# An attention and mixture-of-experts kernel: another guess of the first experts, other planning constants, and a last output cut in two

## The chip, the cores and the metric

The kernel runs on one core of one Trainium2 chip. The metric is the device time of one launch in microseconds (us), the median of several runs. An execution that the hardware profiler recorded is read beside it; its times are counted from the first instruction of its span.

## The reference

Eight batches of 576 tokens with eight heads of 64 columns go through a Nystrom attention with 32 landmarks, and its output rows (4608 of 512 columns) through a mixture of eight experts, one expert for each token.

```
q_lm, k_lm = q, k averaged over 18 neighbouring tokens           # 32 landmarks
A  = softmax(q @ k_lm.T / 8);  Bm = softmax(q_lm @ k_lm.T / 8);  C = softmax(q_lm @ k.T / 8)
Z  = Bm.T / (norm1(Bm) * norminf(Bm) + 1e-6);  six times: Z = 2 Z - Z @ Bm @ Z
x  = (A @ Z @ C @ v), heads side by side                          # (4608, 512)
logits = normalized(x) @ normalized(expert_emb).T / tau           # 8 experts
e  = argmax(logits);  gate = softmax(logits)[e]
out = gate * (relu(x @ w1[e]) @ w2[e])                            # 512 -> 1024 -> 512
```

## The kernel before

All tokens of a batch share one expert in these inputs, and the kernel is built on that. For each batch it guesses one expert, loads only that expert's two weight matrices, and computes the batch with them. It also routes every token exactly, counts the tokens whose expert is another than the guess, and at the very end runs a general path (`general`, under `tc.If` at line 1608) if the count is not zero. In the profiled execution that path did not run.

**A planner orders the work.** Each piece of work (loads, sums, values, queries, landmarks, guess, weights, first and second product of a batch) is a Python generator that announces what it will use next and for how long. The class `Weave` (line 131) plays these announcements against its own clocks, one for each engine, and the order in which it lets generators go on is the order of the instructions on every engine. On the chip each engine runs its instructions strictly in that order, so a planned time acts only through the order it makes. A transfer is taken as landed at the end of its planned share of the queue plus `DMA_LAT`, 3.6 us, whatever the batch (`wv.flag(..., DMA_LAT)`, lines 722, 723, 739, 1361). A group of matmuls may be planned only `MARGIN` (549.6 ns) after its operands, or `BMARGIN` (400 ns) for the two expert products; `SLACK` and `EPS` say how near two candidates must be for their ranks to decide, and `PRI` and `FIRST` hold the ranks.

**Warm matmuls.** Until the first expert product is planned, `keep_warm` (line 668) puts matmuls of a constant of ones (line 673) into the planned gaps of TensorE, so that the engine does not stand still. Their number comes from the planned gaps, too.

**Start.** SP issues the loads of batch 0 (k in two parts, q in two parts, v in two), then those of batch 1. VectorE sums k and q over 18 tokens each (line 762), TensorE starts on the landmarks with these sums, and the attention of batch 0 follows on all engines.

**The guess of batches 0 and 1** (`guess`, line 1168) needs only v. Ten matmuls with a block of ones as stationary operand (128 rows, 32 columns) and the values as moving operand (256 columns, the upper halves of the fp32 numbers read as bf16) sum v over all tokens into one PSUM bank, every sum 32 times over. VectorE transposes the bank (line 1188), multiplies it with the expert embeddings laid out 16 by 8 on each partition (`enB`, line 1193), and `choose` (line 1197) reduces, sums over the partitions with one more matmul, and finds the largest of the eight (line 1216 writes the expert's number). SP then reads that number into a register (line 1340) and issues eight weight transfers of 512 KB (line 1360). Later batches take their guess from the landmarks.

**From weights to the first expert product.** ScalarE squares the four slices of w1 as they land and sums them (line 1374), a power of two is formed from the total (`first_scale`), TensorE multiplies the weights with the batch's landmarks (`first_weights`), ScalarE and VectorE write the scaled result as two fp16 halves (lines 1418, 1420), and `first` (line 1475) multiplies it with the attention weights. `hidden` applies the ReLU (lines 1468, 1470), and `second` (line 1506) multiplies with w2.

**End.** `second` of the last batch takes its small chunk first and four chunks of 128 tokens after it. Each chunk is 24 matmuls of 512 columns into one PSUM bank. `outputs` (line 1540) scales a finished bank on ScalarE or VectorE and SP stores it, 256 KB for a chunk. Before the eviction of the last chunk every engine loads the count of wrong guesses (line 1545).

Of the kernel before, what the change touches and what calls it, by code (L numbers as in the profile page):

```python
# [8 lines left out]
F32 = mybir.dt.float32  # L9
# [42 lines left out]
DMA_LAT = 3600.0  # L52
SLACK = 53.2
EPS = 148.0
MARGIN = 549.6
BMARGIN = 400.0
# [21 lines left out]
PRI = {"loads": 897, "sums": 1694, "inverse": 1697, "values": 1597, "queries": 700, "landmarks": 1656, "rows": 500,  # L78
       "route": 794, "guess": 844, "weights": 803, "first": 550, "second": 550}
# [466 lines left out]
def nystrom_moe(ctx: ExitStack, tc: tile.TileContext, qT, kT, v, emb, w1, w2, out):  # L546
# [77 lines left out]
    con = cst.tile([P, H * E + DM // M * E + 1], F32, name="con")  # L624
# [3 lines left out]
    enB = con[:, H * E:H * E + DM // M * E].rearrange("p (k e) -> p k e", e=E)  # L628
    rtau = con[:, H * E + DM // M * E:]
# [46 lines left out]
    def embeddings():  # L676
# [17 lines left out]
        yield V2(128)  # L694
        vec.tensor_tensor(out=enB, in0=enB, in1=bc(er.unsqueeze(1), [P, DM // M, E]), op=ALU.mult)
# [10 lines left out]
    def loads(b):  # L706
        if b:
            yield "wait", ("loads", b - 1)
        for src, dst, nm in ((kT, kt, "k"), (qT, qt, "q")):
# [6 lines left out]
            for i in range(parts):  # L716
# [3 lines left out]
                for x in range(2 // parts * i, 2 // parts * (i + 1)):  # L720
                    wv.flag((nm, b, x), DMA_LAT)
            wv.flag((nm, b), DMA_LAT)
# [5 lines left out]
    def load_values(b, gg):  # L728
# [10 lines left out]
        wv.flag(("v", b, gg), DMA_LAT)  # L739
# [428 lines left out]
    def guess(b):  # L1168
# [21 lines left out]
        yield "wait", "enB"  # L1190
        pr = wk.tile([P, DM // M, E], F32, name="gpr", bufs=1)
        yield V2(128)
        vec.tensor_tensor(out=pr, in0=bc(tr[:, :, 0:1], [P, DM // M, E]), in1=enB, op=ALU.mult)
        wv.put("half")
# [311 lines left out]
    def second(b):  # L1506
# [5 lines left out]
        for c in order:  # L1512
# [4 lines left out]
            for f in range(8):  # L1517
# [15 lines left out]
                if c == order[-1]:  # L1533
                    wv.put("ht")
                    if f % 2 == 1:
                        wv.put("w2")
# [112 lines left out]
```

## Time and profile before

| | |
|---|---|
| time, median of 3 runs | 449.94 us (449.02 to 450.99) |
| the profiled execution's own time | 449.05 us |
| its span, first to last instruction | 447.3 us |
| TensorE busy | 432.4 us, 97% |
| VectorE busy | 328.1 us, 73% |
| ScalarE busy | 277.5 us, 62% |
| moved by DMA | 78.21 MB, mean 175 GB/s |
| mean granted TensorE clock | 0.995 |

The page calls TensorE's matmuls PE and its weight loads PEld, VectorE DVE, ScalarE ACT, GpSimd POOL and SyncE SP. All matmuls that go through the helper `mm` have its line, 583, so they are told apart by the tiles that they read and write. Warm matmuls have line 673. In a row of the timeline the first two numbers are start and length in us, a bracket at the end is the idle time of the engine before the instruction and what ended it. Busy time of matmuls is merged, so a group's length holds the pipeline's tail after the last start.

### The profile page before, as it was taken

The numbers are of one execution on the slowest core, as the hardware profiler recorded it, in microseconds if no ns is written. First come the engines' busy times: TensorE is split into PE (matmuls) and PEld (weight loads), VectorE is DVE, ScalarE is ACT, GpSimd is POOL, SyncE is SP. The second block draws the span as 40 slices with busy tenths as digits, with TensorE's granted clock in tenths as the row PEclk, the third lists the DMA queues.
The fourth block names the chain that finished last, engine by engine and source line by source line (L and its number), as shares of the span: only waits on it lengthen the run. The fifth ranks groups of instructions, "written<-read, shape, count | busy, mean of one in ns | idle before, by whom it ended". The sixth has DMA issues, their size and how long they took to land.

```text
span 447.3 us, 13932 instructions
## 1 busy us (share of the span) xinstructions
PE 432.4 (97%) x5628; PEld 245.5 (55%) x5628; DVE 328.1 (73%) x1110; ACT 277.5 (62%) x641; POOL 79.5 (18%) x80
## 2 busy tenths in 40 slices
PE   7999989999999999999999999999999999999994
PEld 3454554456555476455565466555665476457541
DVE  4877989988895689987995769765987669455300
ACT  1359645887655865987478648955597457945210
POOL 3042143422241104303230105001310101010000
PEclk9999999999999999999999999999999999999998
DMA  8687644884239816882595249322550219211011
GB/s 291 247 298 245 273 160 150 287 294 142 107 131 313 285 49 211 293 264 79 195 373 178 101 141 366 104 80 114 179 211 26 101 51 359 84 57 38 13 49 52
DMA packets 29705, 78.21 MB, mean 175 GB/s; under 512 B 2625, under 2 KB 14017, under 8 KB 27841
## 3 DMA queue, kind: packets, MB, share of 16 engines
q1 hardware_dynamic: 29488, 77.15, 48.6%
q8 instruction: 46, 0.75, 0.7%
q14 instruction: 27, 0.21, 0.1%
q10 hardware_dynamic: 144, 0.10, 0.1%
HBM read 61.96 MB, written 15.27 MB: 173 GB/s over the span
## 4 chain that ended last, share of the span: by engine, by line
PE 68%; DVE 21%; DMA 3%; ACT 3%; POOL 2%; issue 1%; SPq 1%; POOLq 0%; ACTq 0%; DVEq 0%
PE ps L583 61%; PE ps L673 5%; DVE ht L1470 4%; DVE w2c L1460 3%; DMA k_t<-kT 2%; POOL half L759 2%; DMA wstage<-w 2%; DVE qsum L762 1%; DVE cm L888 1%; PE ps L935 1%; DVE ksum L762 1%; DVE ww L1420 1%; DVE ae L986 1%; DVE asum L997 1%; ACT w2c L1458 1%
## 5 line engine op out<-in xcount | busy, mean ns | idle before, releaser
L583 PE MATMUL ps<-w2c,ht 128*128 128x512 f16 (+1 forms) x1152 | 208.9, 345 | 1.5 <-DVE w2c L1460 1.3
L583 PEld LDWEIGHTS <-ht 128*128 128x128 f16 (+1 forms) x1152 | 88.5, 102 | 79.4 <-issue 7.4
L583 PE MATMUL ps<-ab,ww 128*128 128x288 f16 x768 | 105.4, 286 | 2.2 <-DVE ht L1470 2.1
L583 PEld LDWEIGHTS <-ww 128*128 128x128 f16 x768 | 72.1, 98 | 34.1 <-issue 12.1
L1468 ACT ACTIVATE ht<-ps 128x288 f16<-128x288 f32 x128 | 51.9, 409 | 37.2 <-PE ps L583 36.5
L1470 DVE SCALAR_TENSOR_TENSOR ht<-ps,ht 128x288 f16<-128x288 f32 x128 | 54.7, 447 | 8.8 <-ACT ht L1468 8.5
L1460 DVE SCALAR_TENSOR_TENSOR w2c<-wstage,wsc,w2c 128x1024 f16<-128x1024 f32 x32 | 41.0, 1281 | 12.4 <-ACT w2c L1458 12.4
L1554 ACT ACTIVATE yt<-ps,gfac 128x512 f32<-128x512 f32 (+1 forms) x29 | 18.4, 635 | 46.5 <-PE ps L583 45.9
L1018 POOL TENSOR_TENSOR ae<-ae,am 128x576 f32<-128x576 f32 x15 | 17.3, 1159 | 101.4 <-DVE am L991 81.2
L1458 ACT ACTIVATE w2c<-wstage,wsc 128x1024 f16<-128x1024 f32 x30 | 34.4, 1149 | 0.6 <-PE ps L583 0.2
L1433 ACT ACTIVATE junk<-wstage 128x1024 bf16<-128x1024 f32 x32 | 33.9, 1059 | 0.3
L1374 ACT ACTIVATE junk<-wstage 128x1024 bf16<-128x1024 f32 x32 | 33.8, 1055 | 0.1
L1257 POOL TENSOR_TENSOR nrm<-ssq,half 128x5 f32<-128x5 f32 x8 | 10.0, 1251 | 124.6 <-ACT junk L1239 124.6
L673 PE MATMUL ps<-ones 128*128 128x512 bf16 (+3 forms) x117 | 28.4, 390 | 2.3 <-POOL ones L608 2.3
L1239 ACT ACTIVATE junk<-ps 128x512 bf16<-128x512 f32 (+1 forms) x40 | 23.9, 597 | 10.5 <-DVE lg L1237 9.8
L759 POOL TENSOR_TENSOR half<-k_t 128x576 f32<-128x576 f32 x14 | 18.2, 1302 | 41.2 <-DMA k_t<-kT 18.5
L1418 ACT ACTIVATE ww<-ps,wsc 128x1024 f16<-128x1024 f32 (+1 forms) x18 | 18.2, 1013 | 9.0 <-PE ps L583 9.0
L1420 DVE SCALAR_TENSOR_TENSOR ww<-ps,wsc,ww 128x1024 f16<-128x1024 f32 (+1 forms) x18 | 20.9, 1160 | 3.3 <-ACT ww L1418 3.0
L759 POOL TENSOR_TENSOR half<-q_t 128x576 f32<-128x576 f32 x13 | 17.3, 1332 | 25.5 <-DVE ksum L762 14.5
L583 PE MATMUL ps<-wgd,ab 64*128 64x136 f16 (+1 forms) x480 | 21.1, 221 | 0.6 <-DVE ht L1470 0.4
L583 PEld LDWEIGHTS <-ab 64*128 64x128 f16 (+1 forms) x480 | 14.4, 96 | 12.0 <-issue 11.3
L583 PEld LDWEIGHTS ps<-ek 32*32 32x32 f32 x768 | 12.3, 104 | 15.4 <-issue 6.0
(203 smaller groups left out, 567.8 us busy)
## 6 DMA issues: line engine op xcount, KB each, us to landing
wstage<-w SPq DMA_DIRECT2D x64, 512.0 KB, 6.9
v<-v SPq DMA_DIRECT2D x16, 512.0 KB, 5.1
out<-yt SPq DMA_DIRECT2D x32, 256.0 KB, 2.6
k_t<-kT SPq DMA_DIRECT2D x7, 1152.0 KB, 6.7
q_t<-qT SPq DMA_DIRECT2D x7, 1152.0 KB, 11.9
abs__135<-ab SPq DMA_DIRECT2D x8, 576.0 KB, 3.1
k_t<-kT SPq DMA_DIRECT2D x2, 576.0 KB, 5.6
q_t<-qT SPq DMA_DIRECT2D x2, 576.0 KB
```

Source lines behind the costliest of these rows:

```text
L583: pe.matmul(o, lhsT, rhs, start=start, stop=stop)
L673: pe.matmul(warmth[:, 0:k * P], ones16, bc(ones16.unsqueeze(1), [P, k, P]), start=True, stop=True)
L759: pool.tensor_tensor(out=half, in0=sv[:, :, 0:9], in1=sv[:, :, 9:18], op=ALU.add)
L1239: act.activation(junk[lo:hi, 0:512].rearrange("p (i g x) -> p i g x", i=2, g=2), pfv[:, :, :, 0:2 * D], AF.Square, accum_out=ssq[lo:hi, cg ...
L1374: act.activation(junk, stage[1, b, q], AF.Square, accum_out=sq[:, q:q + 1])
L1420: vec.scalar_tensor_tensor(out=ww[:, 1], in0=pww, scalar=sc, in1=ww[:, 0], op0=ALU.mult, op1=ALU.subtract)
L1433: act.activation(junk, stage[2, b, q], AF.Abs, accum_out=sq[:, q:q + 1])
L1458: act.activation(w[:, 0], st, AF.Copy, scale=sc)
L1460: vec.scalar_tensor_tensor(out=w[:, 1], in0=st, scalar=sc, in1=w[:, 0], op0=ALU.mult, op1=ALU.subtract)
L1468: act.activation(ht[:, 0, r], ph[:, 0:HS], AF.Relu)
L1470: vec.scalar_tensor_tensor(out=ht[:, 1, r], in0=ph[:, 0:HS], scalar=0.0, in1=ht[:, 0, r], op0=ALU.max, op1=ALU.subtract)
L1554: act.activation(yt[:, 0:n], py[:, 0:n], AF.Copy, scale=fac)
```

## The change

It has three parts and a set of constants that go with them.

1. The guess of batches 0 and 1 takes the values as the stationary operand (128 rows, 128 columns, five chunks for each of four column blocks, 20 matmuls) and one column of ones as the moving operand. The sums land with one number per partition, so the transpose goes, and `enB` shrinks from 16 by 8 to 4 by 8 on each partition. The `half` buffer, which the sums on GpSimd use too, is not taken any more.
2. The planner takes the loads of batch 0 (k, q, v and the weights) as landed 2.0 us after their share of the queue, later batches 3.6 us as before. The time that the planner keeps an output buffer (`yt`) after its store goes from 3.6 us to 2.0 us for every batch.
3. The last chunk of the last batch is computed in two halves of 256 columns, 24 matmuls each. The first half's eviction and store are given to the planner as soon as its matmuls are planned. The load of the count of wrong guesses moves to the first half's eviction.

```diff
-DMA_LAT = 3600.0
-SLACK = 53.2
-EPS = 148.0
-MARGIN = 549.6
-BMARGIN = 400.0
+DMA_LAT, DMA_LATE = 2000.0, 3600.0
+SLACK = 46.4
+EPS = 181.8
+MARGIN = 436.5
+BMARGIN = 436.5
 PRI: sums 1694 -> 1697, values 1597 -> 1603, queries 700 -> 703, landmarks 1656 -> 1653,
      route 794 -> 800, first 550 -> 544, second 550 -> 553
+def landing(b):
+    return DMA_LATE if b else DMA_LAT
...
-            wv.flag((nm, b), DMA_LAT)
+            wv.flag((nm, b), landing(b))
...
-        ps_, done = yield from take(T(790, cols=1024, tiles="columns"), 1)
-        for gg in range(2):
-            lead = vt[b, gg].bitcast(BF16).rearrange("p c (x i) -> p c x i", i=2)[:, :, :, 1]
+        ps_, done = yield from take(T(1120, cols=2600), 1)
+        for k in range(4):
+            lead = vt[b, k // 2].bitcast(BF16).rearrange("p c (x i) -> p c x i", i=2)[:, :, :, 1]
             for c in range(5):
-                j = c % 4
-                mm(ps_[32 * j:32 * j + 32, 256 * gg:256 * gg + 256], ones16[:, 0:M], lead[:, c],
-                   start=(c < 4), stop=(c > 0))
+                x = P * (k % 2)
+                mm(ps_[:, k:k + 1], lead[:, c, x:x + P], ones16[:, 0:1], start=(c == 0), stop=(c == 4))
...
-        yield "get", "half"
-        yield VT(512)
-        tr = wk.tile([P, 2 * M, SEG // 2], F32, name="half", bufs=1)
-        tr = tr.rearrange("p m t -> p (m t)")[:, 0:DM].rearrange("p (k r) -> p k r", r=M)
-        vec.transpose(tr.rearrange("p k r -> p (k r)"), ps_)
-        done()
         yield "wait", "enB"
-        pr = wk.tile([P, DM // M, E], F32, name="gpr", bufs=1)
-        yield V2(128)
-        vec.tensor_tensor(out=pr, in0=bc(tr[:, :, 0:1], [P, DM // M, E]), in1=enB, op=ALU.mult)
-        wv.put("half")
+        pr = wk.tile([P, 4, E], F32, name="gpr", bufs=1)
+        yield V(32)
+        vec.tensor_tensor(out=pr, in0=bc(ps_[:, 0:4].unsqueeze(2), [P, 4, E]), in1=enB, op=ALU.mult)
+        done()
...
-            for f in range(8):
+            parts = 2 if (b, c) == (B - 1, order[-1]) else 1
+            n = DM // parts
+            for f, x0 in [(f, n * i) for i in range(parts) for f in range(8)]:
...
-                        mm(py, ht[:, i, o:o + P], w[:, x], start=st_, stop=sp_)
+                        mm(py[:, x0:x0 + n], ht[:, i, o:o + P], w[:, x, x0:x0 + n], start=st_, stop=sp_)
...
+                if parts == 2 and f == 7 and x0 == 0:
+                    wv.add(outputs(b, c, py, None, S * b + o, slice(0, n)), boost=EVICT)
...
-        if (b, c) == (B - 1, 3):
+        if (b, c, cols.start) == (B - 1, 3, 0):
+            yield "wait", "mi"
             left.append(nc.values_load(mi[0:1, 0:1], min_val=0, max_val=NT))
...
-            sp.dma_start(out[t0:t0 + P], yt)
+            sp.dma_start(out[t0:t0 + P, cols], yt[:, 0:n])
```

## Rows read from the trace of the kernel before

**Rows 1.** The page, part 1: busy time, share of span and instructions of each engine.

```profile
PE 432.4 (97%) x5628; PEld 245.5 (55%) x5628; DVE 328.1 (73%) x1110; ACT 277.5 (62%) x641; POOL 79.5 (18%) x80
```

**Rows 2.** Windows: stretch, length, busy us of each engine, clock, DMA share, GB/s.

```profile
60.00:80.00 20.00, 18.19 (x308) 9.04 (x307) 19.15 (x69) 9.25 (x24) 6.51 (x6) 1.00 0.51 172
80.00:120.00 40.00, 39.48 (x620) 22.80 (x619) 34.47 (x110) 31.72 (x77) 12.14 (x10) 1.00 0.65 221
...
440.00:447.30 7.30, 0.96 (x5) 0.23 (x3) 0.00 (x0) 0.69 (x1) 0.00 (x0) 0.71 0.12 42
```

**Rows 3.** Groups by line: the warm matmuls, busy us and mean ns.

```profile
L673 PE MATMUL ps<-ones 128*128 128x512 bf16 (+3 forms) x117 | 28.4, 390 | 2.3 <-POOL ones L608 2.3
```

**Rows 4.** The chain that ended last, in order of time: start, us, what.

```profile
78.01 7.38 DMA wstage<-w
...
345.73 95.24 PE ps L583 x809
```

**Rows 5.** Timeline of the first 23 us: sums, first matmuls, guess of batch 0, weights.

```profile
6.36 7.84 PE L673 MATMUL ps<-ones 128*128 128x512 bf16 x36
...
10.66 2.59 DVE L762 TENSOR_REDUCE qsum<-q_t 128x64 f32<-128x1152 f32 x2
...
14.13 0.27 PE L583 MATMUL ps<-ksum,qsum 64*32 64x32 f32 x13
...
16.44 0.63 PE L583 MATMUL ps<-v,ones 128*32 128x256 bf16 x10
...
17.16 0.71 DVE L1188 STREAM_TRANSPOSE half<-ps 128x512 f32<-128x512 f32 x1
...
17.91 0.28 DVE L1193 TENSOR_TENSOR gpr<-half,con 128x128 f32<-128x128 f32 x1
...
18.23 0.38 DVE L1201 TENSOR_REDUCE gr<-gpr 128x8 f32<-128x128 f32 x1
...
21.32 0.15 DVE L1216 CAST gi<-ge 128x1 int32<-128x1 f32 x1
...
22.53 6.33 SPq L1360 DMA_DIRECT2D wstage<-w  x8
```

**Rows 6.** Timeline, 30 to 42 us: ScalarE's squares of w1 and the first expert product.

```profile
30.97 0.69 ACT L994 ACTIVATE ae<-ae 128x576 f32<-128x576 f32 x1 [2.70 <-POOL ae L1018]
...
34.40 1.04 ACT L1374 ACTIVATE junk<-wstage 128x1024 bf16<-128x1024 f32 x1
...
41.42 1.65 PE L583 MATMUL ps<-ab,ww 128*128 128x288 f16 x12
```

**Rows 7.** Rows nearest to the new guess: one group by form, two matmul groups (timeline).

```profile
L1237 DVE TENSOR_REDUCE lg<-ps 128x8 f32<-128x32 f32 x32 | 5.9, 186 | 10.6 <-PE ps L583 10.5
...
18.40 0.66 PE L935 MATMUL ps<-ident,ec 128*128 128x128 f32 x4
...
37.35 0.53 PE L583 MATMUL ps<-wgd,ab 64*128 64x136 f16 x12
```

**Rows 8.** The end: timeline, ScalarE's half-width group, and page part 6 (KB, us to landing).

```profile
435.86 0.69 ACT L1554 ACTIVATE yt<-ps,gfac 128x512 f32<-128x512 f32 x1 [4.54 <-PE ps L583]
441.04 0.69 ACT L1554 ACTIVATE yt<-ps,gfac 128x512 f32<-128x512 f32 x1 [4.49 <-PE ps L583]
441.76 0.34 SPq L1558 DMA_DIRECT2D out<-yt  x1
...
L1554 ACT ACTIVATE yt<-ps,gfac 128x256 f32<-128x256 f32 x7 | 3.3, 473 | 5.9 <-PE ps L583 5.9
...
abs__135<-ab SPq DMA_DIRECT2D x8, 576.0 KB, 3.1
...
wgs__136<-wgd SPq DMA_DIRECT2D x8, 136.0 KB, 1.7
```

**Rows 9.** Waits of PE, 45 to 441 us: total us, times, longest.

```profile
PE ps L583 <- DVE ht L1470: 2.6, 8, 0.6
...
PE ps L583 <- ACT junk L1239: 0.2, 1, 0.2
```

More of the change, by code (lines that the diff above doesn't have):

```diff
@@ L77 @@
 AHEAD = 20000
-PRI = {"loads": 897, "sums": 1694, "inverse": 1697, "values": 1597, "queries": 700, "landmarks": 1656, "rows": 500,
-       "route": 794, "guess": 844, "weights": 803, "first": 550, "second": 550}
+PRI = {"loads": 897, "sums": 1697, "inverse": 1697, "values": 1603, "queries": 703, "landmarks": 1653, "rows": 500,
+       "route": 800, "guess": 844, "weights": 803, "first": 544, "second": 553}
 FIRST = {"loads": 900, "sums": 800, "inverse": 800, "values": 800, "landmarks": 850, "guess": 810, "weights": 800,
@@ L693, in embeddings @@
         vec.reciprocal(er, er)
-        yield V2(128)
-        vec.tensor_tensor(out=enB, in0=enB, in1=bc(er.unsqueeze(1), [P, DM // M, E]), op=ALU.mult)
+        yield V2(32)
+        vec.tensor_tensor(out=enB, in0=enB, in1=bc(er.unsqueeze(1), [P, 4, E]), op=ALU.mult)
         wv.flag("enB")
@@ L720, in loads @@
                 for x in range(2 // parts * i, 2 // parts * (i + 1)):
-                    wv.flag((nm, b, x), DMA_LAT)
-            wv.flag((nm, b), DMA_LAT)
+                    wv.flag((nm, b, x), landing(b))
+            wv.flag((nm, b), landing(b))
             wv.add(sums(b, nm, dst[b]), boost=rank("sums", b))
@@ L738, in load_values @@
         sp.dma_start(v_t[64:P, 4, :], v[b, 512:576, 256 * gg:256 * gg + 256])
-        wv.flag(("v", b, gg), DMA_LAT)
+        wv.flag(("v", b, gg), landing(b))
         wv.flag(("vload", b, gg))
@@ L1360, in weights @@
             sp.dma_start(st, src[bass.ds(ev, 1), :, 1024 * q:1024 * q + 1024].rearrange("o p x -> (o p) x"))
-            wv.flag(("w", m, b, q), DMA_LAT)
+            wv.flag(("w", m, b, q), landing(b))
         wv.flag(("weights", m, b))
@@ L1532, in second @@
                                start=st_, stop=sp_)
-                if c == order[-1]:
+                if c == order[-1] and x0 + n == DM:
                     wv.put("ht")
@@ L1536, in second, with outputs @@
                         wv.put("w2")
+                if parts == 2 and f == 7 and x0 == 0:
+                    wv.add(outputs(b, c, py, None, S * b + o, slice(0, n)), boost=EVICT)
             wv.flag(("y", b, c))
[L1538 to L1540 removed]
+            wv.add(outputs(b, c, py, done, S * b + o, slice(DM - n, DM)), boost=EVICT)
+    def outputs(b, c, py, done, t0, cols):
         yield "sleep", LAT["pe"]
         yield "wait", ("gfac", b)
[L1543 removed]
+        if (b, c, cols.start) == (B - 1, 3, 0):
+            yield "wait", "mi"
             left.append(nc.values_load(mi[0:1, 0:1], min_val=0, max_val=NT))
         yield "get", "yt"
[L1547 removed]
+        n = cols.stop - cols.start if c < 4 else DM // 2
+        if c == 4:
+            cols = slice(0, n)
         fac = gfac[:, b, c:c + 1]
[L1549 to L1555 removed]
+        who = yield "any", (("act", n / 1.2 + 145), ("dve", (n + 66) / 0.96))
+        yt = wst.tile([P, DM], F32, name="yt", bufs=BUFS["yt"])
+        if who == "dve":
+            vec.tensor_scalar(yt[:, 0:n], py[:, cols], fac, None, op0=ALU.mult)
+        else:
+            act.activation(yt[:, 0:n], py[:, cols], AF.Copy, scale=fac)
+        if done:
+            done()
         yield "use", "dma", 780
         if c < 4:
[L1558 removed]
+            sp.dma_start(out[t0:t0 + P, cols], yt[:, 0:n])
         else:
@@ L1629, in arrays_of @@
         "emb": np.concatenate([np.tile(e.transpose(2, 1, 0).reshape(D, H * E), (2, 1)),
-                               np.tile(blocks.transpose(2, 1, 0).reshape(M, DM // M * E), (4, 1)),
+                               blocks.transpose(2, 1, 0).reshape(P, 4 * E),
                                np.full((P, 1), moe_tau, np.float32)], axis=1),
```

24 lines of the change are left out of this document (8 added, 16 removed).

## The prediction

> **What bounds the kernel now.** Read part 1 of the page first: TensorE is busy 97% of the span, the next engine 73% [rows 1]. That is not all useful work. The groups by line hold 28.4 us of warm matmuls, all of them before the first expert product [rows 3], which starts at 41.42 [rows 6]. Next the windows: from 60 to 80 VectorE is busy 19.15 of 20 us and TensorE idles 1.81; from 80 to 120 TensorE idles 0.52 of 40 us; after its last matmul at 440.96 come 6.34 us of tail [rows 2]. The chain of waits agrees: its last piece is 95.24 us of TensorE without a break up to 441 [rows 4]. So there are three places where time can come from: the start (how early useful matmuls become dense), a few us of waits in between, and the tail. The useful matmuls themselves stay as they are.
>
> At the start the timeline shows TensorE late by plan and not by data. The last sum of q ends at 10.66 + 2.59 = 13.25, but TensorE is in warm matmuls until 14.20 and its first landmark matmul starts at 14.13. The guess's matmuls start at 16.44 with no wait for a transfer [rows 5]. In the planner's count all landings of batch 0 are 1.6 us too late or nearly so.
>
> **Planned landings, batch 0.** Every landing moves 3.6 - 2.0 = 1.6 us earlier in the plan, so fewer warm matmuls stand ahead of the first real one. That matmul cannot start before the last sum: 14.13 - 13.25 = 0.9 us is there; below nothing it cannot go unless a transfer is really later than planned, and then TensorE, DVE or ACT stands at the head of its queue for that transfer, at most the 1.6 us. For the guess I take the whole 1.6 us, since it shows no wait for data: start 16.44 to 14.84. No DMA of batch 0 or 1 is issued in another order by this; SP's eight weight transfers follow the guess at once, behind nothing [rows 5].
>
> **Guess with values stationary.** Removed per guess: a 0.71 us transpose. The multiply shrinks from 0.28 us (128 columns) to at most the 0.19 us of a reduce over 32 columns from PSUM, and the reduce from 0.38 to the same 0.19 [rows 5, 7]: VectorE saves 0.71 + 0.09 + 0.19 = 1.0 us, twice, 2.0 in all. Added: 20 matmuls for 10. The trace has no matmul of this form. Bounds: the ten old ones at (0.63 - 0.28) / 9 = 0.04 us a start give 0.8 us; four fp32 matmuls with 128x128 stationary at (0.66 - 0.27) / 3 = 0.13 give 2.6 us; in fp16 two stationary loads of 128 columns beside each other pass in (0.53 - 0.22) / 5 = 0.062 a pair [rows 5, 7] (0.28, 0.27 and 0.22 are the lengths of single matmuls in those groups). I take the 16-bit row, because the guess reads bf16: 19 x 0.062 + 0.17 = 1.35 us, 0.72 more than 0.63. In batch 0 that replaces warm matmuls; in batch 1 it falls into VectorE's full stretch, where TensorE waits anyway; uncovered it costs 0.7 us there.
>
> For the price of a stationary load the Trainium skill ("TensorE: Matmul & The Clock Gate", LDWEIGHTS (loading the stationary operand)) states its columns over 1.2 per ns, about 107 ns for 128 columns, and in the section on weight-path modes half of that where the load is 128 wide and not fp32. The fp16 pair's 62 ns speaks for the second, the fp32 matmuls' 0.13 us for the first; by the first alone the guess would be 20 x 107 = 2.1 us, an estimate from that page, and the sum below 0.8 us worse.
>
> The expert's number of batch 0, now ready at 21.47 (the cast's end), so comes 1.6 + 0.71 + 0.09 + 0.19 - 0.72 = 1.9 us earlier, and with it the weights, issued at 22.53 now [rows 5].
>
> **Squares of w1.** ScalarE's second square stands behind an exponential that waits 2.70 us for GpSimd; the fourth starts at 34.40 [rows 6]. With weight slices planned 1.6 us earlier some squares go ahead of that exponential. Ends: 0 and 2.7; I take 0.7, near the lower end, because slices still land one after another and an early square can itself wait for its slice with the exponential queued behind it, and GpSimd and VectorE behind that.
>
> **First expert product.** 1.9 + 0.7 = 2.6 us earlier by the weights. By VectorE, which is full until about 80, the check is 0.9 (first sums) + 1.0 + 1.0 (two guesses) = 2.9. The smaller, 2.6, is what the front can give, and what comes late next is VectorE's evictions.
>
> **Last chunk in halves.** Eviction of 256 columns 0.473 for 0.687: -0.21. The store of 128 KB for 256: from 576 KB in 3.1 us and 136 KB in 1.7, 1.4 / 440 a KB, so -0.41; nothing to -0.7 is possible. Matmuls: 12 of 288 columns take (1.65 - 0.29) / 11 = 0.124 a start (0.29 a single one's length), scaled to 256 columns 0.110, 48 of them 5.28; now 24 take the spacing of two evictions, 441.04 - 435.86 = 5.18: +0.10, and +0.77 if 256 columns cost as much as 288 [rows 6, 8]. The first half's eviction, store and the register load lie beside the second half's matmuls; without that cover an eviction and an issue, 0.47 + 0.34. Sum -0.5 us; ends -0.9 and +0.4.
>
> **Constants.** `MARGIN` 549.6 to 436.5 and `BMARGIN` 400 to 436.5, ranks by a few units, `SLACK` and `EPS` reorder everything after the start. TensorE's waits from 45 to 441 are 14 in six rows, 5.5 us in all, first and last row shown [rows 9]. The reorder can give back part of that or add to it; I count 0, with ends -2 (a third of the 5.5) and +3 (13% of the 24.5 us worked out in the rival below). The shorter hold of the output buffers hides behind the 5.18 us between evictions.
>
> **Sum.** -2.6 - 0.5 = -3.1. The profiled execution, 449.05 (447.3 of span and 1.75 around it), becomes about 445.9. The median is 449.94, 0.89 above it, and the forecast for a median is 446.8.
>
> **Rivals.**
>
> *The start's gain is a gap moved.* Batch 1's weights cost the chain 7.38 us of DMA at 78.01 [rows 4]. If batch 1's guess stays where it is in VectorE's queue, TensorE reaches its end of work 2.6 us earlier and waits there. For it: VectorE is the bound in just that stretch [rows 2]. Against: the guess itself gets lighter, and all of VectorE's work ahead of it moves up. Only the tail remains: 449.4.
>
> *Stationary loads bind the guess.* At 0.13 each 2.6 us for 1.35, so 1.3 less at the start: 448.1. For it the fp32 rows, against it the fp16 pair [rows 7]. The Trainium skill's page "TensorE: Matmul & The Clock Gate" stands here with its 107 ns, without the faster mode. It would mean that the second part of the change does little of what it says.
>
> *Planned too near.* With `MARGIN` 113 ns shorter, an attention matmul whose operand is late holds the whole of TensorE's queue, expert products included. About 31 groups a batch, counted in the code, in seven batches are 217; each paying 0.113 us would be 24.5 us. It cancels the gain from 13% of them on and makes the kernel slower by 0.5% from 22%; at 30%, 7.4 us, the time is 446.8 + 7.4 = 454.2. For it: the 14 waits of today, on average 0.4 us [rows 9], show operands that come later than planned by more than the margin. Against: they are 14 of hundreds, and `BMARGIN` grows.
>
> *More than the front.* If the squares get the whole 2.7 us and a third of the 5.5 us of waits goes, about 443.5.
>
> **Chances.** Forecast 0.54 (its own range 445.0 to 448.3), gap moved 0.16, loads bind 0.06, planned too near 0.13, more than the front 0.11. A measurement of this kernel tells about 0.5% from no change, 2.25 us, so 447.7 and 452.2 are the limits. Of the forecast 0.10 lies above 447.7. Faster 0.44 + 0.11 = 0.55; same 0.10 + 0.16 + 0.06 = 0.32; slower 0.13. The range of eight in ten goes from 443.4 to 450.8: it leaves out most of the slower case and the lower part of the last.
>
> **What would show it.** Right: the first landmark matmul about 13.3, the guess's matmuls about 14.8 and 1.4 long, the expert's number near 19.6, the first expert product near 38.8, fewer than 117 warm matmuls, and a span that ends 5.8 us after the last matmul. Wrong in its steps: the guess's matmuls over 2 us; a DVE or ACT wait on a first transfer of over 1 us; TensorE idle between 80 and 120 over 2 us (gap moved); waits of TensorE after 45 above 8 us (planned too near). The forecast as a whole is wrong if the first expert product comes 2 us earlier and the end does not.

## The result and the profile after

The changed kernel takes 445.94 us in the median of four runs (444.8 to 446.45). Four runs of the kernel before on the same chip took 450.47 us (449.02 to 451.58). The ratio is 0.9893, with a 95% interval of 0.9866 to 0.992: faster by 1.1%. The forecast was 446.8 us, inside 443.4 to 450.8, with faster the likeliest sign. The profiled execution took 444.8 us, 443.1 of it span.

TensorE's busy time in part 1 of the page after:

```profile
PE 427.5 (96%) x5653; PEld 245.8 (55%) x5653; DVE 329.6 (74%) x1116; ACT 275.9 (62%) x635; POOL 78.0 (18%) x79
```

Against [rows 1] TensorE is busy 4.9 us less and every other engine as much as before, within 1.6 us. Where the time went can be read by cutting the span at the first expert product. The windows view does that, first for the kernel before, then for the one after (start and end of the stretch, its length, busy us of each engine, granted clock, DMA share, GB/s):

```profile
2.31:41.42 39.11, 38.69 (x492) 18.36 (x493) 29.75 (x100) 16.82 (x43) 7.91 (x14) 1.00 0.79 280
41.42:440.96 399.54, 393.69 (x5144) 227.09 (x5136) 297.70 (x999) 258.88 (x597) 70.01 (x57) 1.00 0.47 167
```

```profile
2.31:39.32 37.01, 35.62 (x495) 17.33 (x496) 29.75 (x99) 17.69 (x45) 7.76 (x14) 1.00 0.79 282
39.32:437.17 397.85, 391.92 (x5166) 228.43 (x5158) 298.62 (x1005) 257.17 (x591) 68.71 (x56) 1.00 0.48 170
```

The start is 2.10 us shorter, the rest up to the last matmul 1.69 shorter, and the tail goes from 447.3 - 440.96 = 6.34 to 443.1 - 437.17 = 5.93. Together that is the 4.2 us of the span. The groups by line give the warm matmuls after:

```profile
L678 PE MATMUL ps<-ones 128*128 128x512 bf16 (+3 forms) x98 | 24.5, 395 | 2.3 <-POOL ones L613 2.3
```

These are 19 matmuls and 3.9 us fewer than in [rows 3]. Without them TensorE did 10.3 us of other matmuls in the start before and 11.1 in the start after, so 0.8 us of work has moved from the rest into the start. The rest idles 5.93 us for 5.85. The remaining 1.0 us of its gain is busy time: the same useful matmuls keep TensorE busy for less time in the other order. No run here shows why.

The timeline of the start after, with the lines that answer to [rows 5]:

```profile
9.28 1.35 DVE L767 TENSOR_REDUCE qsum<-q_t 128x64 f32<-128x1152 f32 x1
10.75 1.33 DVE L767 TENSOR_REDUCE qsum<-q_t 128x64 f32<-128x1152 f32 x1
...
13.40 0.27 PE L588 MATMUL ps<-ksum,qsum 64*32 64x32 f32 x13
...
15.62 0.64 PE L588 MATMUL ps<-ones,v 128*128 128x1 bf16 x20
16.71 0.15 DVE L1191 TENSOR_TENSOR gpr<-ps,con 128x32 f32<-128x32 f32 x1
...
16.90 0.21 DVE L1199 TENSOR_REDUCE gr<-gpr 128x8 f32<-128x32 f32 x1
...
18.94 0.15 DVE L1214 CAST gi<-ge 128x1 int32<-128x1 f32 x1
...
20.14 2.08 SPq L1358 DMA_DIRECT2D wstage<-w  x4
```

The landmarks start at 13.40 for 14.13, the guess's matmuls follow 2.2 us later as they did before, and the number is there at 19.09 for 21.47. The last sum of q, which ended at 13.25 before, ends at 12.08, so it does not hold the landmarks. One execution fixes such a start to about a microsecond only: in the six experiments below that keep this order up to here, the landmarks start between 12.39 and 13.37. The same view of ScalarE, VectorE and GpSimd, for [rows 6]:

```profile
25.50 1.04 ACT L1372 ACTIVATE junk<-wstage 128x1024 bf16<-128x1024 f32 x1
...
30.50 1.16 POOL L1023 TENSOR_TENSOR ae<-ae,asum 128x576 f32<-128x576 f32 x1 [0.62 <-DVE scw L1131]
30.75 0.19 ACT L1372 ACTIVATION_READ_ACCUMULATOR junk<-wstage 128x1 f32 x1
...
31.21 0.48 DVE L1150 CAST wgd<-wen 128x16 f16<-128x16 f32 x1
31.62 1.30 POOL L764 TENSOR_TENSOR half<-k_t 128x576 f32<-128x576 f32 x1
...
31.73 1.23 DVE L1152 TENSOR_TENSOR wgd<-wen,wgd 128x16 f16<-128x16 f32 x1
32.88 0.14 DVE L1376 TENSOR_REDUCE wsq<-wsq 128x1 f32<-128x4 f32 x1
...
39.32 1.65 PE L588 MATMUL ps<-ab,ww 128*128 128x288 f16 x12
```

All four squares of w1 are done at 30.94; before, the last ended at 35.54. VectorE adds them up only at 32.88, because two small instructions ahead in its queue end together with GpSimd's instructions and not after their own 0.1 to 0.2 us. What that costs the first expert product, here 2.1 us earlier, is tested below (e10_port).

The windows of batch 1, for [rows 2]:

```profile
60.00:80.00 20.00, 17.56 (x249) 7.39 (x248) 18.79 (x62) 12.00 (x27) 9.85 (x8) 1.00 0.79 279
80.00:120.00 40.00, 39.61 (x639) 24.19 (x638) 35.29 (x127) 26.99 (x69) 8.21 (x7) 1.00 0.46 166
```

VectorE still fills 60 to 80, TensorE now idles 2.44 us there, and 0.39 from 80 to 120. Batch 1's number comes at a very different time, as its timeline row shows:

```profile
59.45 0.12 DVE L1214 CAST gi<-ge 128x1 int32<-128x1 f32 x1
60.43 5.74 SPq L1358 DMA_DIRECT2D wstage<-w  x7
```

Before, the number came at 74.37 and the weights were issued from 75.34 on. The transfer of 7.38 us at 78.01 in the chain [rows 4] is gone; a transfer of weights of 7.39 us stands in the chain after at 127.66. Between 59.6 and 79 that chain runs mostly through VectorE and GpSimd, and its last pieces are these (start, us, what):

```profile
383.81 50.28 PE ps L588 x411
434.71 2.47 PE ps L588 x21
```

The break between them is new. The end in the timeline, for [rows 8]:

```profile
431.21 0.69 ACT L1560 ACTIVATE yt<-ps,gfac 128x512 f32<-128x512 f32 x1 [4.54 <-PE ps L588]
434.17 0.48 DVE L1558 TENSOR_SCALAR yt<-ps,gfac 128x256 f32<-128x256 f32 x1 [18.14 <-PE ps L588]
434.71 2.45 PE L588 MATMUL ps<-w2c,ht 128*128 128x256 f16 x21 [0.64 <-DVE yt L1558]
437.26 0.48 DVE L1558 TENSOR_SCALAR yt<-ps,gfac 128x256 f32<-128x256 f32 x1 [2.60 <-PE ps L588]
```

TensorE stands for 0.64 us between the halves, because the second half writes into the bank that the first half's eviction still reads (e2_ownbank, below, takes another bank, and the wait is gone). TensorE's waits from 45 us to the end (total us, times, longest), to compare with [rows 9]; the seven rows together are 5.1 us, for 5.5 before:

```profile
PE ps L588 <- DVE ek L1080: 1.4, 2, 1.1
...
PE ps L588 <- DVE yt L1558: 0.6, 1, 0.6
```

### The profile page after: what moved, and what is told of

The parts are those of the page before. It is cut to its first block, busy times and chain, and to the rows that moved or that the text cites. A ratio compares the mean times of both kernels' runs of the same rounds, so it can differ in the third digit from the quotient of the medians.

```text
span 443.1 us, 13980 instructions
## 1 busy us (share of the span) xinstructions
PE 427.5 (96%) x5653; PEld 245.8 (55%) x5653; DVE 329.6 (74%) x1116; ACT 275.9 (62%) x635; POOL 78.0 (18%) x79
## 4 chain that ended last, share of the span: by engine, by line
PE 69%; DVE 21%; ACT 3%; POOL 3%; issue 2%; DMA 2%; SPq 0%; DVEq 0%; POOLq 0%
PE ps L588 63%; PE ps L678 4%; DVE ht L1468 3%; DVE w2c L1458 2%; POOL half L764 2%; DMA wstage<-w 2%; DVE ae L991 1%; PE ps L940 1%; DVE qsum L767 1%; DVE am L996 1%; DVE cm L893 1%; DVE asum L1002 1%; DVE at L1008 1%; ACT junk L1372 1%; DVE ab L1013 1%
## 5 line engine op out<-in xcount | busy, mean ns | idle before, releaser
L588 PE MATMUL ps<-w2c,ht 128*128 128x512 f16 (+2 forms) x1176 | 208.4, 341 | 1.4 <-DVE w2c L1458 0.8
L588 PEld LDWEIGHTS <-ht 128*128 128x128 f16 (+1 forms) x1176 | 90.9, 102 | 77.7 <-issue 7.7
L1560 ACT ACTIVATE yt<-ps,gfac 128x512 f32<-128x512 f32 (+1 forms) x26 | 16.3, 629 | 31.7 <-PE ps L588 31.6
L1456 ACT ACTIVATE w2c<-wstage,wsc 128x1024 f16<-128x1024 f32 x29 | 33.2, 1146 | 1.5 <-PE ps L588 1.3
L1023 POOL TENSOR_TENSOR ae<-ae,am 128x576 f32<-128x576 f32 x13 | 15.0, 1157 | 76.8 <-DVE am L996 75.4
L1558 DVE TENSOR_SCALAR yt<-ps,gfac 128x512 f32<-128x512 f32 (+1 forms) x15 | 10.4, 695 | 24.3 <-PE ps L588 24.3
L678 PE MATMUL ps<-ones 128*128 128x512 bf16 (+3 forms) x98 | 24.5, 395 | 2.3 <-POOL ones L613 2.3
L588 PE MATMUL ps<-ek 32*32 32x64 f32 (+1 forms) x768 | 19.8, 216 | 1.3 <-DVE ek L1080 1.1
```

The source lines that it names most:

```text
L588: pe.matmul(o, lhsT, rhs, start=start, stop=stop)
L678: pe.matmul(warmth[:, 0:k * P], ones16, bc(ones16.unsqueeze(1), [P, k, P]), start=True, stop=True)
L1456: act.activation(w[:, 0], st, AF.Copy, scale=sc)
```

## The experiments

Two theories stood against each other. By the first, each part of the change gives a time of its own, and the parts add: about 2 us by the lighter guess and the earlier landings, some tenths by the halves, nothing by the constants. By the second, the theory of the order (O in the expectations), the parts give little by themselves. The order of the 400 us behind the first expert product is what decides, and the constants were chosen for exactly one set of announced costs.

The table has all runs. "First product" is the start of the first expert product, "rest" the time from there to the end of the last matmul, "idle" TensorE's idle time between its first matmul at 2.31 and its last, "tail" what follows, all from one profiled execution each. The median and the ratio to the kernel before (with its interval) are of the timed runs.

| kernel | first product | rest | idle | tail | median | ratio |
|---|---|---|---|---|---|---|
| before | 41.42 | 399.5 | 6.3 | 6.3 | 450.47 | |
| after | 39.32 | 397.9 | 7.3 | 5.9 | 445.94 | 0.9893 [0.9866, 0.992] |
| e1_whole | 40.20 | 398.1 | 9.2 | 6.3 | 445.29 | 0.9901 [0.9871, 0.9931] |
| e2_ownbank | 39.00 | 397.4 | 6.7 | 6.0 | 444.01 | 0.9878 [0.9847, 0.9909] |
| e3_oldguess | 39.37 | 408.9 | 14.1 | 6.0 | 455.18 | 1.0124 [1.0093, 1.0156] |
| e4_late | 40.23 | 404.8 | 13.6 | 7.0 | 453.08 | 1.0076 [1.0051, 1.0101] |
| e5_guessonly | 40.19 | 409.7 | 16.7 | 6.3 | 458.22 | 1.0165 [1.0107, 1.0222] |
| e6_landonly | 39.15 | 408.0 | 12.3 | 6.4 | 453.77 | 1.0076 [1.0038, 1.0113] |
| e7_oldconst | 39.17 | 403.4 | 10.3 | 5.9 | 449.77 | 0.9986 [0.9959, 1.0013] |
| e8_newconst | 40.77 | 405.5 | 12.1 | 6.4 | 454.35 | 1.0093 [1.0062, 1.0124] |
| e9_sameorder | 38.56 | 401.7 | 9.2 | 6.0 | 447.9 | 0.9943 [0.991, 0.9977] |
| e10_port | 38.00 | 398.2 | 6.8 | 5.9 | 445.56 | 0.9892 [0.9864, 0.9919] |
| e11_port_own | 38.17 | 398.0 | 6.7 | 6.1 | 444.9 | 0.9877 [0.9846, 0.9909] |
| e12_margin | 38.68 | 399.9 | 8.4 | 5.9 | 446.89 | 0.9927 [0.9897, 0.9956] |

The kernel before had medians of 448.88 beside e1 to e4, 450.78 beside e5 to e8 and 450.82 beside e9 to e12. These three groups ran on three chips, so across groups the ratio is the better measure. It is not the quotient of the two medians.

### The last chunk: whole, and the second half in a bank of its own

The edit of e1_whole, in the kernel after:

```diff
-            parts = 2 if (b, c) == (B - 1, order[-1]) else 1
+            parts = 1
```

> The changed kernel with the last chunk in one piece again (24 matmuls of 512 columns, one eviction, one store). Theory A, from the trace of the changed kernel: the second half's matmuls wait 0.64 us for the first half's eviction, and what the smaller eviction (0.21) and store save is less than that wait, so the cut gains nothing: time equal to the changed kernel or 0.1 to 0.5 us below it, the end of the last matmul to the end of the span about 6.3 us again instead of 5.9. Rival B, as forecast: the cut is worth 0.5 us, so this kernel is 0.5 us slower than the changed one.

The edit of e2_ownbank, also in the kernel after:

```diff
+            banks = [(py, done)]
             for f, x0 in [(f, n * i) for i in range(parts) for f in range(8)]:
+                if x0 and f == 0:
+                    banks.append((yield from take(None, 1, "py")))
+                py, done = banks[-1]
...
-                    wv.add(outputs(b, c, py, None, S * b + o, slice(0, n)), boost=EVICT)
+                    wv.add(outputs(b, c, py, done, S * b + o, slice(0, n)), boost=EVICT)
```

> The changed kernel with the second half of the last chunk in a PSUM bank of its own, taken when the first half is done, so that it need not wait for the first half's eviction. Theory A: the wait of 0.64 us goes, nothing else moves, and the time is 0.6 us below the changed kernel. Rival B: the 0.64 us is TensorE waiting for something else (its queue, the load of the count of wrong guesses), and stays: no difference.

With the last chunk whole the ratio is 0.9901, with it in halves 0.9893: the halves as they were made gain nothing that can be measured. In a bank of its own the second half follows without a break. The timeline of e2_ownbank has the eviction before the cut chunk and the last one; its windows show TensorE full up to the last matmul at 436.40, with 24 matmuls of 256 columns in 2.60 us:

```profile
431.24 0.69 ACT L1564 ACTIVATE yt<-ps,gfac 128x512 f32<-128x512 f32 x1 [4.54 <-PE ps L588]
...
436.49 0.48 DVE L1562 TENSOR_SCALAR yt<-ps,gfac 128x256 f32<-128x256 f32 x1 [2.14 <-PE ps L588]
...
433.80:436.40 2.60, 2.60 (x24) 2.08 (x22) 0.48 (x1) 0.00 (x0) 0.00 (x0) 1.00 0.19 58
```

From the one eviction to the other 436.49 - 431.24 = 5.25 us pass. In after it is 437.26 - 431.21 = 6.05, and a whole chunk took 5.18 [rows 8]. So the break costs 0.80 us, a little more than the 0.64 that TensorE is seen to wait. With the tails of 5.9 and 6.0 us for 6.3, the halves in one bank come out about 0.5 us behind the whole chunk by these rows, and those in two banks about 0.3 ahead.

The timed runs can hardly resolve this. e2_ownbank is 1.3 us faster than e1_whole on the same chip (444.01 and 445.29), and e11_port_own, below, is 0.7 faster than e10_port in the same way; both go the right way, but the intervals overlap. e2_ownbank has the lowest median of all kernels here, 1.2% below the kernel before, and by the ratio e11_port_own equals it.

### One part taken out: the old guess, the old landings, the old constants

e3_oldguess puts the guess of before back, with the announcements, the `half` buffer and the embedding layout of before; the rest is the kernel after:

```diff
-        ps_, done = yield from take(T(1120, cols=2600), 1)
-        for k in range(4):
...
+        ps_, done = yield from take(T(790, cols=1024, tiles="columns"), 1)
+        for gg in range(2):
...
+        yield "get", "half"
+        yield VT(512)
...
+        vec.transpose(tr.rearrange("p k r -> p (k r)"), ps_)
```

> The changed kernel with the guess of the kernel before (10 matmuls with ones stationary, transpose on VectorE, embeddings 16 by 8 on each partition); planned landings, constants and halves as in the changed kernel. Theory A: the guess gives about half of the earlier start: expert number of batch 0 near 20 us instead of 19.1, first expert product near 40.2 instead of 39.3, and the time 1 to 2 us above the changed kernel. Rival B: batch 1's guess decides, because its expert number falls back from about 60 to about 74 us: time 3 us or more above. Rival C: the guess is hidden and the planned landings give all: within 0.5 us.

e4_late takes back the earlier landings:

```diff
-    return DMA_LATE if b else DMA_LAT
+    return DMA_LATE
```

> The changed kernel with the planned landing of batch 0's transfers back at 3.6 us (output buffers still held 2.0 us in the plan). Theory A: the first sums and the guess stand behind warm matmuls again: guess's matmuls near 16.4 instead of 15.6, first expert product near 41 instead of 39.3, warm matmuls about 3 us more, time 1.5 to 2 us above the changed kernel. Rival C: the start is bound by the work of VectorE and the weights' DMA, not by the plan: within 0.5 us of the changed kernel.

e7_oldconst has the constants and ranks of before in the kernel after:

```diff
-SLACK = 46.4
-EPS = 181.8
-MARGIN = 436.5
-BMARGIN = 436.5
+SLACK = 53.2
+EPS = 148.0
+MARGIN = 549.6
+BMARGIN = 400.0
...
```

> The changed kernel with the constants of the kernel before (SLACK, EPS, MARGIN, BMARGIN and the ranks); guess, landings and halves as changed. Theory S: the parts give their gain by themselves, time within 1 us of the changed kernel, 3 to 4 us below the kernel before. Theory O: the first expert product still comes near 39.5 us, but batch 1's expert number falls back towards 74 us, TensorE's idle time in the middle is above 10 us, and the time is above the kernel before.

e3_oldguess and e4_late end above the kernel before, at 455.18 and 453.08, and e7_oldconst, at 449.77, cannot be told from it. In none is the gain lost at the start. Their first expert product comes at 39.2 to 40.2, 1.2 to 2.3 us before that of the kernel before. They lose it in the rest, which grows from 397.9 to between 403.4 and 408.9. The windows of e7_oldconst show it best, since it differs from after by constants alone:

```profile
2.31:39.17 36.86, 35.19 (x484) 16.91 (x484) 28.65 (x98) 16.81 (x42) 6.29 (x12) 1.00 0.80 291
39.17:442.55 403.38, 394.75 (x5178) 228.11 (x5170) 297.53 (x1001) 262.02 (x596) 74.16 (x60) 1.00 0.47 167
```

Its start is as good as after's, 36.86 us for 37.01. Its rest has 8.63 us of idle time for 5.93 and 2.8 more of busy time. Batch 1's number comes at 58.0, earlier still than the 59.45 of after, so an early number is not enough.

Whether a late number loses the time was rival B of e3_oldguess. Its signs came: the number is at 74.2 and the time far more than 3 us above after. The other runs speak against a late number as the whole cause. It is at 72.7 to 75.0 in e4_late, e6_landonly and e8_newconst as well, and at 64.6 in e5_guessonly, the slowest; but in the kernel before it is at 74.4, and that kernel is faster than all five. The theories A of e3_oldguess and e4_late, 1 to 2 us for the part itself, fall.

In e3_oldguess the largest waits are on the hidden layer and the scaled weights, with single ones of 2.0 and 2.8 us:

```profile
PE ps L588 <- DVE ht L1476: 4.7, 8, 2.0
PE ps L588 <- DVE w2c L1466: 3.9, 3, 2.8
```

Behind the longest one the granted clock falls from 1.00 to 0.50, the lower of the two levels (the matmuls behind the wait, then one of the windows of a microsecond):

```profile
184.65 4.87 PE L588 MATMUL ps<-w2c,ht 128*128 128x512 f16 x14 [2.80 <-DVE w2c L1466]
...
186.00:187.00 1.00, 1.00 (x3) 0.30 (x2) 1.00 (x4) 0.61 (x1) 1.00 (x1) 0.50 0.00 0
```

Fourteen matmuls take 4.87 us there; at full clock 24 of them take 5.18 [rows 8], so 14 would take 3.0, and the fall costs about 1.8 us (an estimate from these rows). The same fall is in e5_guessonly at 64, in e6_landonly at 61 and at 167, and in e8_newconst at 73, each time behind waits of about 1 to 3 us. It is not in the kernels before and after, and not in e4_late and e7_oldconst, which wait as well; what brings it is not shown. So in four of the six slow kernels, e3 to e8, a part of the loss is not waiting but slower matmuls behind the waits.

### One part alone in the kernel before

e5_guessonly is the kernel before with the new guess; its edit is that of e3_oldguess the other way round:

```diff
-        ps_, done = yield from take(T(790, cols=1024, tiles="columns"), 1)
...
+        ps_, done = yield from take(T(1120, cols=2600), 1)
...
+                mm(ps_[:, k:k + 1], lead[:, c, x:x + P], ones16[:, 0:1], start=(c == 0), stop=(c == 4))
...
```

> The kernel before with only the new guess (values stationary, no transpose); planned landings, constants and last chunk as before. Theory S (the parts add up): expert number of batch 0 about 0.8 us earlier, first expert product up to 0.8 us earlier, 2 us less work on VectorE, time 1 us below the kernel before. Theory O (each part reorders the whole plan, and waits in the middle decide): the start is 0.5 to 1 us earlier all the same, but TensorE's idle time between first and last matmul, 6.3 us before and 7.3 after, moves by several us, and the time with it, most likely above the kernel before, as in the two runs where one part was taken out.

e6_landonly is the kernel before with the earlier landings and the shorter hold of `yt`:

```diff
-DMA_LAT = 3600.0
+DMA_LAT, DMA_LATE = 2000.0, 3600.0
...
-            wv.flag((nm, b), DMA_LAT)
+            wv.flag((nm, b), landing(b))
```

> The kernel before with only the planned landing of batch 0 at 2.0 us (and the output buffers' hold, which has the same constant). Theory S: guess and first sums 0.8 us earlier, some of ScalarE's squares ahead of the exponential, first expert product 1 to 1.5 us earlier, time 1 to 1.5 us below the kernel before. Theory O: start earlier by the same, idle time of TensorE in the middle above 10 us, time 2 to 8 us above the kernel before.

e8_newconst is the kernel before with the constants and ranks of after, the edit of e7_oldconst the other way round:

```diff
-MARGIN = 549.6
-BMARGIN = 400.0
+MARGIN = 436.5
+BMARGIN = 436.5
...
```

> The kernel before with only the constants of the changed one. Theory S: within 1.5 us of the kernel before, since ranks and margins change by little. Theory N (the shorter MARGIN is what gains): 1.5 to 3 us below it. Theory O: start unchanged (first expert product near 41.4), idle time of TensorE in the middle above 10 us, time 3 to 9 us above the kernel before.

All three are slower than the kernel before, by 1.7%, 0.8% and 0.9%, though the first expert product is earlier in all of them, at 40.19, 39.15 and 40.77. The rest takes 409.7, 408.0 and 405.5 us. In e6_landonly one row holds most of the waiting:

```profile
PE ps L588 <- DVE ht L1475: 8.6, 7, 2.7
```

In all six slow kernels the waiting lies in the middle: from the first expert product to 240 us TensorE idles 7.4 to 14.4 us, for 5.7 before and 5.2 after, and from 240 on at most 1.2 us in any of them.

The theory of adding parts falls. It needs gains that sum to about 4.5 us, and the runs have three losses of 3 to 7.4.

### The same order with the old guess's instructions

e9_sameorder separates the guess's work from the order. The planner is told the costs of the new guess, so all other instructions keep the order of after, but what is issued is the old guess, with its transpose into a buffer of its own:

```diff
+            for c in range(5):
+                j = c % 4
+                mm(ps_[32 * j:32 * j + 32, 256 * gg:256 * gg + 256], ones16[:, 0:M], lead[:, c],
...
+        tr = wk.tile([P, DM // M, M], F32, name="gtr", bufs=1)
+        vec.transpose(tr.rearrange("p k r -> p (k r)"), ps_)
+        vec.tensor_tensor(out=pr, in0=bc(tr[:, :, 0:1], [P, DM // M, E]), in1=enB, op=ALU.mult)
```

> The order of instructions planned for the changed kernel, but the guess's own instructions are the old ones (10 matmuls, transpose, multiply and reduce over 128 columns, embeddings 16 by 8, in a tile of their own): on every other engine the sequence is that of the changed kernel. It measures what the guess's instructions cost with the reorder taken out. Theory O (the 9 us of the run with the old guess came from another order, not from the guess's work): expert number of batch 0 about 1 us later than the changed kernel's 18.9, time 1 to 2.5 us above the changed kernel, 446.5 to 448.5. Theory W (the work itself costs that much, since VectorE is full up to 80 us): 6 us or more above, near 453.

In the trace every engine runs the same sequence as in after, apart from the guess and the layout of its embeddings. The time is 447.9, with a wide spread (444.79 to 451.02). So about 455.18 - 447.9 = 7.3 us of e3_oldguess's loss are order, with what the `half` buffer may add, which only e3_oldguess shares with GpSimd. Theory W, 6 us or more for the guess's work, falls.

The 2 us that are left between e9_sameorder and after are not shown to be the price of the guess's work. In the profile the old guess costs 0.6 us of batch 0's time: from the first landmark matmul to the cast that writes the number 6.11 us pass, for 5.54 in after.

```profile
14.70 0.63 PE L588 MATMUL ps<-v,ones 128*32 128x256 bf16 x10
15.69 0.67 DVE L1193 STREAM_TRANSPOSE gtr<-ps 128x512 f32<-128x512 f32 x1
...
16.40 0.29 DVE L1194 TENSOR_TENSOR gpr<-gtr,con 128x128 f32<-128x128 f32 x1
```

A number later than after's did not show, since this execution began its landmarks at 12.39 and not at 13.40. Its first expert product, 38.56, is earlier than after's too. What makes it slower than after's profiled execution (447.94 for 444.80) is a single wait of 2.28 us before the matmul at 237.16, for which the profile shows no cause, and TensorE's lower clock behind it. The windows of one microsecond (length, busy us of the engines, granted clock, DMA share, GB/s):

```profile
236.00:237.00 1.00, 0.00 (x0) 0.00 (x0) 0.00 (x0) 0.00 (x0) 0.00 (x0) 1.00 1.00 354
237.00:238.00 1.00, 0.84 (x22) 0.56 (x27) 0.00 (x0) 0.00 (x0) 0.08 (x1) 0.65 1.12 282
238.00:239.00 1.00, 1.00 (x23) 0.19 (x8) 0.00 (x0) 0.00 (x0) 1.00 (x1) 0.50 1.05 316
239.00:240.00 1.00, 1.00 (x29) 0.83 (x26) 0.30 (x2) 0.89 (x1) 0.21 (x1) 0.50 0.41 97
240.00:241.00 1.00, 1.00 (x11) 0.38 (x7) 0.59 (x3) 1.00 (x2) 0.00 (x0) 0.65 0.06 18
```

The four windows at 0.65, 0.50, 0.50 and 0.65 lack 1.7 us of full clock, so wait and clock cost about 4.0 us (an estimate from these rows), and without them this execution would have taken 444, no more than after. Its time is also the median of the runs. Whether the stop has to do with the old guess is open; so in this order the guess's instructions cost between nothing and 2 us.

### VectorE's two small instructions beside GpSimd

e10_port lets the two instructions that ended with GpSimd's read PSUM instead of a buffer in SBUF; the planner is told the same as before, so the order stays:

```diff
+        vec.tensor_scalar(wd[:, :, 0, 2 * D:], pg, scw[:, b:b + 1], None, op0=ALU.mult)
+        vec.scalar_tensor_tensor(out=wd[:, :, 1, 2 * D:], in0=pg, scalar=scw[:, b:b + 1], in1=wd[:, :, 0, 2 * D:],
...
-        vec.tensor_copy(wd[:, :, 0, 2 * D:], wen)
-        vec.tensor_tensor(out=wd[:, :, 1, 2 * D:], in0=wen, in1=wd[:, :, 0, 2 * D:], op=ALU.subtract)
```

> The changed kernel in the same order, but two small VectorE instructions of each batch (the fp16 halves of the expert logits' weights, 16 columns) read the PSUM bank instead of a copy in SBUF. In the trace of the changed kernel the two took 0.48 and 1.23 us at 31.2 to 33.0 in batch 0 (0.17 and 0.12 before), ending with GpSimd's instructions. Theory P (they wait for GpSimd, and the start hangs on them): each about 0.3 us, first expert product 1 to 1.5 us earlier (near 38), time 0.5 to 1.5 us below the changed kernel. Rival: the same stretches stay long from PSUM too, or the start gain is lost in the middle; within 0.4 us of the changed kernel.

e11_port_own has this edit and that of e2_ownbank together.

> Both repairs together: the two VectorE instructions from PSUM, and the second half of the last chunk in a bank of its own. If both act, their gains add, since one lies in the start and one in the tail: 1.1 to 2.1 us below the changed kernel, about 443 to 444, and below both kernels. If the first repair does nothing, the time is that of the kernel with the bank alone, 444.0.

They compute the same values from the bank, so their form changes too. The two now take 0.22 and 0.23 us, while GpSimd works beside them as before:

```profile
30.01 1.16 POOL L1023 TENSOR_TENSOR ae<-ae,asum 128x576 f32<-128x576 f32 x1 [0.62 <-DVE scw L1131]
...
30.60 0.22 DVE L1146 TENSOR_SCALAR wgd<-ps,scw 128x16 f16<-128x16 f32 x1
...
30.86 0.23 DVE L1147 SCALAR_TENSOR_TENSOR wgd<-ps,scw,wgd 128x16 f16<-128x16 f32 x1
31.01 0.14 DVE L1377 TENSOR_REDUCE wsq<-wsq 128x1 f32<-128x4 f32 x1
```

That GpSimd's neighbourhood stretches them, and not their form, shows in e7_oldconst. There the two are unchanged, GpSimd has ended at 33.08, and they take 0.16 and 0.17 us; beside GpSimd in e1_whole, e2_ownbank and e12_margin it is 0.48 and 1.22 to 1.23 again:

```profile
33.62 0.16 DVE L1150 CAST wgd<-wen 128x16 f16<-128x16 f32 x1
...
33.81 0.17 DVE L1152 TENSOR_TENSOR wgd<-wen,wgd 128x16 f16<-128x16 f32 x1
```

The sum of squares starts at 31.01 for 32.88, and the first expert product at 38.00 for 39.32. Of these 1.32 us, 0.68 is an earlier start of this execution (its first landmark matmul is at 12.72). The sum of squares gains 1.2 us beyond that, but from it to the first expert product 6.99 us pass for 6.44, so the repair is worth 0.6 us there. The profiled execution keeps the earlier start (443.82 for 444.80, with a rest of 398.2 for 397.9). The timed runs show nothing of it: the ratios of e10_port and after are 0.9892 and 0.9893, those of e11_port_own and e2_ownbank 0.9877 and 0.9878, and e11_port_own missed its 443 to 444. A gain of 0.6 us is below what the runs of one kernel differ by, so whether it reaches the end is open.

### A neighbouring margin

e12_margin moves `MARGIN` and `BMARGIN` from 436.5 to 450.0 in the kernel after:

```diff
-MARGIN = 436.5
-BMARGIN = 436.5
+MARGIN = 450.0
+BMARGIN = 450.0
```

> The changed kernel with MARGIN and BMARGIN at 450.0 instead of 436.5 ns, nothing else. Theory O (the constants pick out one order, and its neighbours are worse by chance): start as in the changed kernel up to about 39 us, then another order, idle time of TensorE 3 us or more above the changed kernel's 7.3, time 2 to 8 us above. Theory N (the size of the margin matters, not the order it happens to give): 13.5 ns are nothing, within 0.7 us of the changed kernel.

It takes 446.89, ratio 0.9927: 1 us worse than after by the medians, with the intervals overlapping. Both theories miss, O with 2 to 8 us and N with 0.7. The traces show that the order is not a new one from the start: TensorE's matmuls write and read the same tiles, one after another, for the first 2377 of 5653, up to 166.54 us in e12_margin and 167.49 in after, and VectorE's and ScalarE's instructions agree as far. (e7_oldconst leaves after's order behind the 139th matmul.) The shared stretch from the first expert product takes 127.9 us here and 128.2 in after. Where the orders differ the lengths do too, first e12_margin, then after:

```profile
166.54:438.53 271.99, 268.83 (x3278) 156.40 (x3275) 185.81 (x613) 168.55 (x381) 39.48 (x33) 1.00 0.41 148
```

```profile
167.49:437.17 269.68, 267.77 (x3277) 156.79 (x3276) 186.81 (x620) 168.38 (x379) 33.87 (x28) 1.00 0.42 149
```

So this run does not speak against the order. It keeps after's order through most of the stretch in which e3 to e8 lose their time, and what it loses, 2.3 us in these rows, comes behind that. How far one step of a margin redraws the order is what theory O had wrong.

## Why the prediction was right

**The start** gave 2.1 us where 2.6 were forecast, by other terms than planned. The first landmark matmul is at 13.40 (forecast 13.3), though its floor, the last sum of q, moved as well. The guess's matmuls came 0.82 us earlier and not 1.6, because the 2.2 us between the landmarks and the guess stayed; in the other executions of this order they are at 14.87 to 15.59, so the forecast's 14.8 is within reach of the scatter. The guess itself costs 0.64 us and not 1.35: 20 pairs of a stationary load and a matmul of one column at (0.64 - 0.16) / 19 = 0.025 us a start, 0.16 being a single matmul's length. That is below the lower bound of 0.8 in the prediction, and the rival in which the loads bind is refuted. The term was mis-sized because the fp16 pair that priced it has 136 moving columns. At the 0.124 us of 288 columns [rows 6], 0.43 ns a column, these alone take 58 of the 62 ns, so that row told the price of its columns and not of its loads. The two errors nearly cancel: the number came at 19.09 for a forecast of 19.6. The squares gained more than the 0.7 us counted, 4.6 - 2.4 = 2.2 beyond the number's own lead. VectorE's two small instructions then took 0.48 + 1.23 - 0.17 - 0.12 = 1.4 us of it back, by GpSimd's work beside them; e10_port, without that, has the first expert product 0.6 us earlier.

**The tail** is the step that was wrong. The evictions (0.48 for 0.69) and the matmuls (0.108 a start in e2_ownbank, forecast 0.110) are as worked out, and the span ends 5.93 us after the last matmul (forecast 5.8). The prediction said that the first half's eviction lies beside the second half's matmuls. It does not: both use one bank, TensorE waits 0.64 us, and the break costs 0.80. For a forecast of -0.5 us the rows give about +0.5 in after, just beyond the end of +0.4, and -0.3 with a second bank.

**The gap moved** is refuted by its own sign: TensorE idles 0.39 us from 80 to 120, and batch 1's number came 15 us earlier, not 2.6. The prediction's picture of batch 1, VectorE's queue with the same order moved up, was too simple, since the whole order was made anew.

**The constants** were counted as 0, with ends of -2 and +3, and here the sum came out by luck. With the old constants the other parts are worth 0.14% (e7_oldconst, an interval that holds 1), some 0.6 us where the start and the tail were forecast at 3.1. With the new ones they are worth 1.1%, so in this company the constants bring about 4 us, twice the end of -2. Without the parts the same constants cost 0.9% (e8_newconst). Neither term has a size of its own, and two errors of opposite sign gave a sum near the measured one.

The prediction gave a slower outcome a chance of 0.13, for a margin that is too short. Waits like those that it described come with the shorter margin and the old parts (e8_newconst idles 12.1 us), but as much with the old and longer one (16.7 in e5_guessonly, 12.3 in e6_landonly), and with the shorter one in after they do not come. So the margin alone does not bring them.

**More than the front** had half its conditions: the squares got nearly their 2.7 us, but TensorE's waits stayed at 5.1 us. The time lies between this case and the forecast. (By its own terms, 2.0 us more for the squares and a third of 5.5, that case comes to 443.0 and not 443.5.)

So the forecast rested on the start's gain being kept by the 400 us behind it, with the new order there counted as 0. In after it is kept. In six of the twelve experiments, e3 to e8, it is not, with a first expert product 0.7 to 2.3 us before that of the kernel before. What in the order decides that is open. Batch 1's early number, the most visible difference, is in e7_oldconst too and is not enough there.

## What to carry to other kernels

In a kernel whose order a planner makes, a part of a change has no price of its own: measure the whole, and take a part's price only from a run in which the order is held fixed while the instructions change. Compare the sequences of the two traces before an order is called the same or a new one. An early start is worth only what the stretch behind it keeps, so look at the time from the first dense work to the last beside the time of the start. A tile that is drained in halves needs a bank for each half, or its producer waits for the first drain.

## What the runs showed of the hardware

Stationary loads of 128 columns in bf16, each with a matmul of one column, start 25 ns apart (20 in 0.64 us). The 62 ns of the fp16 pairs in [rows 7], with 136 moving columns, are no price of a load.

Small VectorE instructions between buffers in SBUF can end together with the GpSimd instruction beside them: 0.17 us became 0.48 and 0.12 became 1.23 in after, while in e7_oldconst, with GpSimd idle, the two took 0.16 and 0.17. The same values computed from PSUM took 0.22 and 0.23 us beside GpSimd's work (e10_port).

Behind the wait of 2.28 us in e9_sameorder the granted clock was 0.50 in the windows from 238 to 240, the lower of the two levels, where it had been 1.00 up to 237. Behind the wait of 2.80 us in e3_oldguess it was 0.50 as well, and 14 matmuls of 512 columns took 4.87 us.
